# Gated attention and two expert mixtures on one core: the first mixture by 512 tokens in a written order, the early heads of a pair as one 128x128 block

## The chip, the core and the metric

One core of one Trainium2 chip runs the kernel. The metric is the device time of one execution in microseconds. Before the change the median of three runs is 990.67 us (990.52 to 990.67). One profiled execution took 989.96 us; the trace and all durations in this document come from it, or from the profiled execution of the kernel that is named.

## The reference

Three layers follow each other. The weights of the first mixture arrive as 64-bit floating-point words; the output is float32.

```python
# 1. gated linear attention: 4 batches, 8 heads, 768 tokens, 48 channels
for t in range(768):
    state = alpha[:, :, t, :, None] * state + k[:, :, t] (x) v[:, :, t]   # outer product
    y[:, :, t] = q[:, :, t] . state
x = y as 3072 tokens x 384
# 2. first mixture: 384 -> 768 -> 384
x = max(x @ w1, x @ w2, x @ w3) @ w_out
# 3. second mixture: 8 experts, the two best of each token
logits = x @ w_gate + log1p(exp(x @ w_noise)) * noise
out[token] += softmax weight * (relu(x @ w1[e]) @ w2[e])   # 384 -> 1024 -> 384
```

## The kernel before

**Attention.** A half unit j (24 of them) is 256 tokens of four heads: two pairs of heads, one head of a pair on partitions 0 to 47, the other on 64 to 111, with 16 padding partitions above each. The 256 tokens are four chunks of 64. `prep_a` runs two scans on VectorE over the decays (a reverse one for `kh`, then a forward one for `D`, which needs the reciprocals of the first) and GpSimd multiplies the keys; `prep_x` multiplies the queries by `D`, one VectorE operation for each height (`x1`, `x2`; L258, L259). `att_t` transposes the keys, `att_s` makes the scores and masks them with two VectorE multiplies (L293). `att_g` makes the outer sums in the bank `psG`, puts the last state into its column 0 (L311 clears it for the first in a sequence), scans over it (L316), multiplies by the decay (L319) and copies the states beside the values (`LA`, `LB`). `att_y` gets the outputs, two matmuls with 64 rows of output for each chunk, and splits them into a high and a low part (`xt`); six small DMAs (`xt<-sg`) fill the rows 48 to 63 and 112 to 127 of them.

**First mixture.** Two half units make a unit u of 256 tokens. `ffn(u, f)` does one of six blocks of 128 hidden channels: for each of three weights nine matmuls of 256 columns (three slices of the depth, each as high x high, high x low, low x high). The first two weights go into one bank (tag `p12`), the third into another (`p3`), two buffers of each. ScalarE copies the first (L366), VectorE takes two maxima (L367, L368), ScalarE and GpSimd split the result into `H`. `proj(u, t)` multiplies 128 tokens by `w_out` and by the gates (18 matmuls of 400 columns, `psl`). The weights come as 64-bit words; `wconv(i)`, twelve times, turns them into two float32 parts in `dissect`: ScalarE takes the absolute value (L163), VectorE does four operations (a maximum with a tiny number L164, a shift L165, and two that put sign and low bits in, L166 and L167), ScalarE and GpSimd make the high and low part (L169, L170). It uses two work tiles, `ca` and `cb`, with two buffers each.

**Second mixture.** `route_a` to `route_m` find the two experts of six tiles of tokens at a time (four batches) and write a table of token numbers. `eload` loads an expert's weights, `esplit` splits them (L738, L739), `gather` fetches rows by an indirect DMA, `turn` transposes them (L773) and copies them into `xe` (L775), `up` and `down` are the two products (L792 with 384 or 448 columns, L806 with 384), `scatter` adds the rows to the output by indirect DMA.

**What sets the order.** The calls stand in a written list in the code: the attention of the first units, the weight conversions and the first blocks one by one, then a loop over the units 3 to 11, then the last projections and the first expert. Within the reach of the list a scheduler with modelled times puts each engine's instructions in order, and the buffers of each tag bound how far it can move them. The calls between the last blocks of the first mixture and the third transpose of the expert's second part are called the handover here.

## Time and profile before

| | of the profiled execution |
|---|---|
| its own time; span of the trace | 989.96 us; 988.3 us |
| TensorE matmuls (PE), weight loads (PEld) | 913.0 us (92%), 866.7 us (88%) |
| VectorE (DVE) | 514.6 us (52%) |
| ScalarE (ACT) | 389.5 us (39%) |
| GpSimd (POOL) | 329.3 us (33%) |
| granted TensorE clock, mean of the span | 0.98 of 2.4 GHz |
| moved by DMA | 88.22 MB, mean 89 GB/s |

The span runs from the first instruction to the last; the 1.66 us that the execution takes beside it are not in the trace. An engine's busy share is an average over stages that have different limits. In the first 120 us TensorE is busy in 69.2 us and VectorE in 110.4, from 120 to 480 TensorE in 356.3 of 360 and VectorE in 236.3. So the table of stages is read before the shares.

### The profile page before, as it was taken

Reading aid. Unit: us, or ns where it says so; the run is one execution under the profiler, and the core shown is the slowest. Engines: PE = TensorE matmul, PEld = TensorE weight load, DVE = VectorE, ACT = ScalarE, POOL = GpSimd, SP = SyncE. Lnnn points to the kernel's source line nnn. Section 1 sums busy time; section 2 is a strip of 40 time slices with the busy share of each in tenths; the row PEclk is TensorE's granted clock in tenths of the full one; section 3 lists DMA queues with packets and bytes.
Section 4 is the critical chain, followed back from the end, with each engine's and each line's share of the span. In section 5 each row is a group of like instructions: output and inputs, shape, how many; then the busy total and the mean of one; then the engine's idle time right before and its main releaser. Section 6 shows DMA issues by size and latency. Waiting matters only on the chain.

```text
span 988.3 us, 17871 instructions
## 1 busy us (share of the span) xinstructions
PE 913.0 (92%) x7186; PEld 866.7 (88%) x7187; DVE 514.6 (52%) x1040; ACT 389.5 (39%) x801; POOL 329.3 (33%) x362
## 2 busy tenths in 40 slices
PE   2358999999999999999898999999999999999994
PEld 2347999999999999999897999999999999999993
DVE  7999847786668865772573333322333323333110
ACT  3645454455445534632542333332333332333220
POOL 5477524322322332112108333333333233221112
PEclk9979899999999999999999999999999999999998
DMA  9642223134234232104325444334434434422112
GB/s 266 171 137 70 60 55 87 46 106 121 57 82 122 75 81 64 31 13 137 139 87 123 113 105 101 78 79 115 110 98 108 94 60 109 113 57 25 21 25 29
DMA packets 36693, 88.22 MB, mean 89 GB/s; under 512 B 8640, under 2 KB 25024, under 8 KB 36608
## 3 DMA queue, kind: packets, MB, share of 16 engines
q1 hardware_dynamic: 25600, 66.39, 23.7%
q0 software_dynamic: 11008, 20.67, 12.0%
q8 instruction: 57, 0.93, 0.4%
q14 instruction: 28, 0.23, 0.1%
HBM read 64.52 MB, written 20.16 MB: 86 GB/s over the span
## 4 chain that ended last, share of the span: by engine, by line
PE 74%; issue 4%; DMA 3%; DVE 2%; POOL 0%; ACT 0%; POOLq 0%; ACTq 0%; DVEq 0%
PE psd L806 21%; PE psu L792 21%; PE p L363 18%; PE psl L378 5%; DMA out_dram<-y,idx 2%; PE psx L773 2%; PE psS L290 1%; PE psG L306 1%; PE psY L331 1%; PE psT L282 1%; DMA xt<-sg 1%; PE psY L332 1%; DVE kh L239 0%; DVE x L259 0%; DMA xg<-x2d,idx 0%
## 5 line engine op out<-in xcount | busy, mean ns | idle before, releaser
L363 PE MATMUL p<-xt,W 128*128 128x256 f32 x1944 | 254.7, 289 | 9.9 <-DVE m L367 7.3
L363 PEld LDWEIGHTS p<-xt,W 128*128 128x128 f32 x1944 | 241.9, 195 | 15.0 <-DVE m L367 8.1
L792 PE MATMUL psu<-xe,ew 128*128 128x448 f32 (+1 forms) x1152 | 242.5, 358 | 4.3 <-ACT xe L775 4.3
L806 PE MATMUL psd<-ew,he 128*128 128x384 f32 (+1 forms) x1344 | 243.3, 335 | 0.0
L806 PEld LDWEIGHTS psd<-ew,he 128*128 128x128 f32 (+1 forms) x1344 | 227.0, 180 | 8.1 <-ACT y L809 0.2
L792 PEld LDWEIGHTS psu<-xe,ew 128*128 128x128 f32 x1152 | 208.2, 190 | 13.9 <-ACT xe L775 4.7
L796 DVE SCALAR_TENSOR_TENSOR he<-psu,he 128x448 fp32r<-128x448 f32 (+1 forms) x128 | 75.5, 590 | 265.0 <-ACT he L795 265.0
L811 POOL DMA_INDIRECT out_dram<-y,idx x56 | 88.1, 1573 | 187.8 <-ACT y L809 176.2
L371 POOL TENSOR_TENSOR H<-m,H 128x256 fp32r<-128x256 f32 x72 | 60.1, 835 | 191.2 <-ACT H L370 187.1
L809 ACT ACTIVATE y<-psd,GS 128x384 f32<-128x384 f32 (+1 forms) x56 | 32.4, 580 | 206.1 <-PE psd L806 195.2
L795 ACT ACTIVATE he<-psu 128x448 fp32r<-128x448 f32 (+1 forms) x128 | 66.3, 518 | 112.3 <-PE psu L792 112.3
L378 PE MATMUL psl<-WO,H 128*128 128x400 f32 x432 | 84.7, 349 | 0.0
L378 PEld LDWEIGHTS psl<-WO,H 128*128 128x128 f32 x432 | 76.7, 188 | 2.1 <-issue 1.3
L739 DVE TENSOR_TENSOR ew<-raw,ew 128x768 fp32r<-128x768 f32 x64 | 57.2, 954 | 33.6 <-ACT ew L738 32.9
L758 POOL DMA_INDIRECT xg<-x2d,idx x56 | 58.5, 1045 | 43.2 <-PE psx L773 21.2
L367 DVE TENSOR_TENSOR m<-p,m 128x256 f32<-128x256 f32 x72 | 29.9, 417 | 60.4 <-ACT m L366 59.9
L370 ACT CAST H<-m 128x256 fp32r<-128x256 f32 x72 | 29.2, 406 | 68.0 <-DVE m L368 66.2
L777 POOL COPY GS<-xg 128x1 f32<-128x1 f32 (+1 forms) x56 | 10.8, 272 | 124.2 <-DMA xg<-x2d,idx 124.2
L366 ACT COPY m<-p 128x256 f32<-128x256 f32 x72 | 26.4, 369 | 61.6 <-PE p L363 58.4
L738 ACT CAST ew<-raw 128x768 fp32r<-128x768 f32 x64 | 48.6, 831 | 3.2 <-DMA raw<-in_e_dram 3.2
L331 PE MATMUL psY<-x,la 128*64 128x64 f32 x384 | 31.5, 237 | 15.6 <-ACT la L321 14.9
L331 PEld LDWEIGHTS psY<-x,la 128*64 128x64 f32 x384 | 27.1, 148 | 19.7 <-ACT la L321 15.7
(151 smaller groups left out, 1080.0 us busy)
## 6 DMA issues: line engine op xcount, KB each, us to landing
raw<-in_e_dram SPq DMA_DIRECT2D x32, 768.0 KB, 5.6
qka<-in_qka_dram SPq DMA_DIRECT2D x48, 289.7 KB, 4.7
out_dram<-z SPq DMA_DIRECT2D x5, 960.0 KB, 4.5
vn<-in_vn_dram SPq DMA_DIRECT2D x24, 192.0 KB, 2.6
x2d<-x2t SPq DMA_DIRECT2D x24, 192.0 KB, 1.9
RAW<-in_ws_dram SPq DMA_DIRECT2D x5, 768.0 KB, 10.8
wraw<-in_ws_dram SPq DMA_DIRECT2D x4, 768.0 KB, 8.6
xt<-sg SPq DMA_DIRECT2D x72, 32.0 KB, 3.5
```

Of the source, the lines that this page charges most:

```text
L331: nc.tensor.matmul(ps[0:64, p, s], LA[i][:, p, c], X1[j][:, sx], start=True, stop=True)
L363: nc.tensor.matmul(ps, W[:, f, w, a, k], x[:, k, b], start=n == 0, stop=n == 8)
L371: nc.gpsimd.tensor_sub(H[:, u % 2, f, 1], m, hi.bitcast(F32))
L378: nc.tensor.matmul(ps, H[:, u % 2, f, a, 128 * t:128 * t + 128], WOT[0][:, b, f], start=n == 0, stop=n == 17)
L738: nc.scalar.copy(hi, r)
L739: nc.vector.tensor_sub(EW[e, m][:, 1, s], r, hi.bitcast(F32))
L758: nc.gpsimd.indirect_dma_start(out=XG[n, i][0:w], out_offset=None, in_=x2d if h else x2d[0:128 + LATE], in_offset=bass.IndirectOffsetOnAxi ...
L792: nc.tensor.matmul(ps, w[:, a, f, k], XE[n][:, k, b], start=i == 0, stop=i == 8)
L795: nc.scalar.activation(hi, ps, AF.Relu)
L796: nc.vector.scalar_tensor_tensor(HE[n][:, f, 1], ps, 0.0, hi.bitcast(F32), op0=OP.max, op1=OP.subtract)
L806: nc.tensor.matmul(ps, HE[n][:, f, a, o:o + m], w[:, b, f], start=j == 0, stop=j == 23)
L811: nc.gpsimd.indirect_dma_start(out=out, out_offset=bass.IndirectOffsetOnAxis(ap=IDX[h][0:m, 1, c:c + 1], axis=0), in_=y, in_offset=None, c ...
```

## The change

**Attention.** `EARLY = 4`: in the half units 0 to 3 the pair's two heads are one block. One tile `L[0]` holds the values, both heads on the diagonal, and one tile `L[1]` the states; an output chunk is two matmuls of 128 rows that add up in the bank (masked scores by values, decayed queries by states). So one multiply of full height makes the queries (L294 for L258 and L259), and one mask multiply the scores. In all half units the decay scan now starts from the decay of the last step (`Z[0]`) and comes first, the reverse scan second. `att_g` adds the old state into column 1 and one scan adds and multiplies, so the multiply by the decay goes; ScalarE spreads the factors `AE`. The inputs of the first two half units come as three pieces of columns with the padding inside (`qk2`), the decays first; the values have a load of their own (`load_v`).

**Weights.** The maximum of `dissect` moves to GpSimd, and the work tile is one, in place, with two buffers. Raw weights have other homes.

**First mixture.** `ffn(d, f, half)` works on groups of 512 tokens. Group 0 and the blocks 0 and 1 of group 1 run in halves of 256 columns, all else with 512. Each of a block's three products has a bank of its own, of one tag `p` with four buffers, which `up` uses too. `proj(d, t)` has four tiles of 128 tokens in a group.

**Routing and order.** Batches of 6, 6, 6, 2 and 4 tiles instead of four times 6. The order of the calls is written as two strings, in which `f1.0.1` is `ffn(1, 0, 1)` and `r` one step of the routing; at the handover a third string sets it and the scheduler does not move TensorE, VectorE and ScalarE.

```diff
+EARLY = 4
+BATCH = (0, 6, 12, 18, 20, 24)
+HANDOVER = """
+    L0.0.0 L0.0.1 L0.1.0 G0.0 G0.1 G0.2 E0.0.0 E0.0.1 p5.0 E0.0.2 E0.0.3 p5.1 T0.0 T0.1 T0.2 E0.1.0 E0.1.1
...
+ORDER = """
+    a0 x0 t0 a1 s0 v0 g0 x1 s1 a2 t1 y0 v1 x2 g1 a3 y1 w0 v2 w1 w2 t2 s2 x3 g2 v3 w3 w4 t3 s3 y2 g3 a4
...
     def load(j):
         i = j % 2
-        for g in range(2):
-            nc.sync.dma_start(QKA[i][64 * g:64 * g + 48], qka[j, g])
-        nc.sync.dma_start(VN[i].rearrange("p a b c e -> p (a b c e)"), vn[j])
+        if j < 2:
+            for a, b in ((1024, 1545), (512, 1024), (0, 512)):
+                nc.sync.dma_start(QKA[i][:, a:b], qk2[j, :, a:b])
...
     def dissect(raw, hi, lo):
-        a = at.tile([128, 768], U32, tag="ca", name="ca", bufs=2)
-        b = at.tile([128, 768], F32, tag="cb", name="cb", bufs=2)
+        b = cv.tile([128, 768], F32, tag="cb", name="cb", bufs=2)
+        a = b.bitcast(U32)
         nc.scalar.activation(b, high.bitcast(F32), AF.Abs)
-        nc.vector.tensor_scalar(b, b, TINY, None, op0=OP.max)
-        nc.vector.tensor_scalar(a, b.bitcast(U32), 5, 2, op0=OP.logical_shift_left, op1=OP.logical_shift_right)
+        nc.gpsimd.tensor_scalar(b, b, TINY, None, op0=OP.max)
+        nc.vector.tensor_scalar(a, a, 5, 2, op0=OP.logical_shift_left, op1=OP.logical_shift_right)
...
     def prep_a(j):
+        nc.vector.tensor_copy(Z[0][:, 0:512:64], a0)
+        D = DD[j] = at.tile([128, 512], F32, tag="D", name="D")
+        nc.vector.tensor_tensor_scan(D, al[:, 0:512], Z[0], 0.0, op0=OP.mult, op1=OP.add)
+        nc.vector.reciprocal(Z[1][:, 63:512:64], D[:, 63:512:64])
         R = KH[j] = at.tile([128, 512], F32, tag="kh", name="kh", bufs=2)
-        nc.vector.memset(Z[:, 0:512:64], 1.0)
-        nc.vector.tensor_tensor_scan(R[:, ::-1], al[:, 512:0:-1], Z, 0.0, op0=OP.mult, op1=OP.add)
-        nc.vector.reciprocal(Z[:, 0:512:64], R[:, 0:512:64])
-        D = DD[j] = at.tile([128, 512], F32, tag="D", name="D")
-        nc.vector.tensor_tensor_scan(D, al[:, 0:512], Z, 0.0, op0=OP.mult, op1=OP.add)
-        r0 = at.tile([128, 2, 4], F32, tag="r0", name="r0")
-        nc.gpsimd.tensor_copy(r0.rearrange("p a b -> p (a b)"), R[:, 0:512:64])
+        nc.vector.tensor_tensor_scan(R[:, ::-1], al[:, 512:0:-1], Z[1][:, ::-1], 0.0, op0=OP.mult, op1=OP.add)
         nc.gpsimd.tensor_mul(R, t[:, 512:1024], R)
-        nc.gpsimd.tensor_mul(AE[i][:, :, :, 1:5],
-                             a0.rearrange("p (a b) -> p a b", a=2)[:, :, None, :].to_broadcast([128, 2, 48, 4]),
-                             r0[:, :, None, :].to_broadcast([128, 2, 48, 4]))
+        EN[j] = at.tile([128, 2, 4], F32, tag="en", name="en", bufs=2)
+        nc.vector.tensor_copy(EN[j].rearrange("p a b -> p (a b)"), D[:, 63:512:64])
...
+    def bank(j, name, early=False):
+        if early and j < 4:
+            return pm.tile([128, 512], F32, tag="p", name=name, bufs=4)
+        return pa.tile([128, 512], F32, tag="a", name=name)
...
     def att_s(j):
+        if j < EARLY:
+            nc.vector.tensor_mul(X2[j].rearrange("p (c t) -> p c t", c=8), ps.rearrange("p (c t) -> p c t", c=8),
+                                 mask[:, None, :].to_broadcast([128, 8, 64]))
+            return
...
     def att_g(j):
+        nc.scalar.copy(AE[:, :, :, 1:5], EN[j][:, :, None, :].to_broadcast([128, 2, 48, 4]))
...
+        nc.vector.memset(ps[:, :, :, 0], 0.0)
+        if not first:
+            before = ST[j - 2][:, :, :, 4]
+            nc.scalar.copy(LA[i][64:128, :, 0, 0:48], before[64:128])
+            nc.scalar.copy(LB[i][0:64, :, 0, 0:48], before[0:64])
+            nc.vector.tensor_add(ps[:, :, :, 1], ps[:, :, :, 1], before)
+        nc.vector.tensor_tensor_scan(st.rearrange("q p e c -> q (p e c)"), ps.rearrange("q p e c -> q (p e c)"),
+                                     AE.rearrange("q p e c -> q (p e c)"), 0.0, op0=OP.add, op1=OP.mult)
-        nc.vector.tensor_mul(st[:, :, :, 0:4], st[:, :, :, 0:4], AE[i][:, :, :, 1:5])
...
+    def att_y_mm(j):
+                for k, X in enumerate((X2, X1)):
+                    nc.tensor.matmul(ps[:, p, sc], L[k][:, p, c], X[j][:, sx], start=k == 0, stop=k == 1)
...
-    def ffn(u, f):
-        p12 = pm.tile([128, 2, 256], F32, tag="p12", name="p12")
-        p3 = pm.tile([128, 2, 256], F32, tag="p3", name="p3")
+    def ffn(d, f, half=None):
+        s = slice(0, 512) if half is None else slice(256 * half, 256 * half + 256)
+        x = XT[d][:, :, :, s]
+        m = pw.tile([128, 512], F32, tag="m", name="m", bufs=2)[:, s]
+        for w in range(3):
+            ps = pm.tile([128, 512], F32, tag="p", name="p", bufs=4)[:, s]
...
+            if w == 0:
+                nc.scalar.copy(m, ps)
+            else:
+                nc.vector.tensor_max(m, ps, m)
...
+    with tc.manual_schedule(engines={mybir.EngineType.PE, mybir.EngineType.DVE, mybir.EngineType.Activation}):
+        run(HANDOVER)
```

VectorE from its 20th instruction or so on, when the first weights are converted; a row gives the line, the operation, and output<-input with their shape (`cb` and `ca` are the work tiles, `x` the queries or masked scores, `st` the states). Before:

```order
L164 TENSOR_SCALAR cb<-cb 128x768
L293 TENSOR_TENSOR x_155<-psS,mask 64x512
L293 TENSOR_TENSOR x_156<-psS,mask 64x512
L165 TENSOR_SCALAR ca<-cb 128x768
L311 MEMSET psG 128x96
L164 TENSOR_SCALAR cb<-cb 128x768
L166 SCALAR_TENSOR_TENSOR ca<-wraw,ca 128x768
L316 SCALAR_TENSOR_TENSOR st<-ae_105,psG 128x480
L165 TENSOR_SCALAR ca<-cb 128x768
L167 SCALAR_TENSOR_TENSOR ca<-wraw,ca 128x768
L164 TENSOR_SCALAR cb<-cb 128x768
L319 TENSOR_TENSOR st<-st,ae_105 128x96x4
```

The same place after:

```order
L294 TENSOR_TENSOR x_209<-qka_99,D 128x512
L340 TENSOR_TENSOR x_149<-psS,mask 128x512
L368 MEMSET psG 128x96
L375 SCALAR_TENSOR_TENSOR st<-psG,ae 128x480
L208 TENSOR_SCALAR cb<-cb 128x768
L209 SCALAR_TENSOR_TENSOR cb<-RAWH,cb 128x768
L340 TENSOR_TENSOR x_210<-psS,mask 128x512
L210 SCALAR_TENSOR_TENSOR cb<-RAWH,cb 128x768
L208 TENSOR_SCALAR cb<-cb 128x768
L209 SCALAR_TENSOR_TENSOR cb<-RAWH,cb 128x768
L210 SCALAR_TENSOR_TENSOR cb<-RAWH,cb 128x768
```

A conversion has three operations there instead of four, the mask is one row of full height, and the multiply of the states has gone.

TensorE at the handover, from the last blocks of the first mixture (`p`, L363) over the last projections (`psl`), the transposes (`psx`) and the first expert's products (`psu`, `psd`). Before:

```order
L363 MATMUL p_5828<-xt,W 128x256 x9
L378 MATMUL psl_5879<-WO,H 128x400 x3
L378 MATMUL psl_5902<-WO,H 128x400 x15
L773 MATMUL psx<-ident,xg 128x128 x6
L378 MATMUL psl_5925<-WO,H 128x400 x18
L378 MATMUL psl_5955<-WO,H 128x400 x18
L773 MATMUL psx<-ident,xg 128x128 x3
L792 MATMUL psu<-xe_5988,ew 128x384 x36
```

The same place after, up to the routing's first matmul (`psr`):

```order
L466 MATMUL psl_5017<-WO,H 128x400 x11
L466 MATMUL psl_5047<-WO,H 128x400 x18
L728 MATMUL psx<-ident,xg 128x128 x9
L466 MATMUL psl_5099<-WO,H 128x400 x18
L466 MATMUL psl_5128<-WO,H 128x400 x18
L747 MATMUL psu<-xe_5070,ew 128x384 x27
L538 LDWEIGHTS tri
L538 MATMUL psr<-r_ob,tri 128x32
```

All nine transposes stand ahead of the last two projections there, and the routing's matmuls come after the third up block. Further down, before the second part's transposes:

```order
L610 MATMUL pstab<-r_C,r_A 128x192
L747 MATMUL psu<-xe_5070,ew 128x384 x9
L761 MATMUL psd<-ew,he_5183 128x384 x48
L728 MATMUL psx<-ident,xg 128x128 x6
L761 MATMUL psd<-ew,he_5183 128x384 x24
L728 MATMUL psx<-ident,xg 128x128 x3
```

The eighth up block and two down blocks stand between the routing's last matmul (`pstab`, into the table of token numbers) and the next transposes.

## Rows read from the trace of the kernel before

**Rows 1.** Stages: window, us, busy (count) PE, PEld, DVE, ACT, POOL, clock, DMA, GB/s.
```profile
0.00:60.00 60.00, 22.14 (x251) 19.61 (x253) 52.92 (x70) 28.03 (x49) 33.28 (x44) 0.94 0.75 204
60.00:120.00 60.00, 47.06 (x463) 44.35 (x462) 57.48 (x76) 29.06 (x60) 38.74 (x28) 0.86 0.31 79
120.00:480.00 360.00, 356.27 (x3743) 339.83 (x3742) 236.31 (x567) 163.97 (x375) 103.82 (x127) 1.00 0.29 75
480.00:540.00 60.00, 52.94 (x291) 48.84 (x290) 34.69 (x115) 26.17 (x51) 18.06 (x26) 0.94 0.46 137
540.00:960.00 420.00, 420.00 (x2363) 400.75 (x2362) 133.15 (x215) 139.97 (x264) 129.28 (x136) 1.00 0.37 84
```
**Rows 2.** Timeline, VectorE, 8 to 15 us: start, us, operation, idle before.
```profile
8.57 1.23 DVE L239 TENSOR_TENSOR_SCAN kh<-qka,Z 128x512 f32<-128x512 f32 x1 [5.22 <-DMA qka<-in_pad_dram]
10.07 1.23 DVE L242 TENSOR_TENSOR_SCAN D<-qka,Z 128x512 f32<-128x512 f32 x1
```
**Rows 3.** Groups, VectorE, 0 to 111 us: busy us, mean ns, idle before.
```profile
L242 DVE TENSOR_TENSOR_SCAN D<-qka,Z 128x512 f32<-128x512 f32 x7 | 13.3, 1902 | 0.1
L165 DVE TENSOR_SCALAR ca<-cb 128x768 uint32<-128x768 uint32 x11 | 8.5, 776 | 0.0
L166 DVE SCALAR_TENSOR_TENSOR ca<-wraw,ca 128x768 uint32<-128x768 uint32 x6 | 8.1, 1359 | 0.0
L164 DVE TENSOR_SCALAR cb<-cb 128x768 f32<-128x768 f32 x11 | 8.0, 723 | 0.0
L259 DVE TENSOR_TENSOR x<-qka,D 64x512 f32<-64x512 f32 x6 | 7.9, 1309 | 0.1
L258 DVE TENSOR_TENSOR x<-qka,D 64x512 f32<-64x512 f32 x6 | 7.0, 1173 | 0.2
L293 DVE TENSOR_TENSOR x<-psS,mask 64x512 f32<-64x512 f32 x10 | 6.8, 682 | 0.1
L316 DVE TENSOR_TENSOR_SCAN st<-ae,psG 128x480 f32<-128x480 f32 x5 | 5.7, 1141 | 0.1
L167 DVE SCALAR_TENSOR_TENSOR ca<-wraw,ca 128x768 uint32<-128x768 uint32 x6 | 5.7, 944 | 0.0
L319 DVE TENSOR_TENSOR st<-st,ae 128x384 f32<-128x384 f32 x5 | 4.5, 892 | 0.0
L240 DVE RECIPROCAL Z<-kh 128x8 f32<-128x8 f32 x7 | 1.4, 196 | 0.1
```
**Rows 4.** Chain of work that ended last: start, us, what.
```profile
347.99 5.97 DMA xt<-sg
...
460.12 19.45 PE p L363 x162
...
655.74 4.18 PE psd L806 x24
659.92 5.30 PE psu L792 x27
...
938.46 3.71 PE psu L792 x18
```
**Rows 5.** Groups, ScalarE, 0 to 111 us, columns as in rows 3.
```profile
L169 ACT CAST W<-ca 128x768 fp32r<-128x768 f32 x9 | 7.5, 835 | 8.2 <-DVE ca L167 8.1
L163 ACT ACTIVATE cb<-wraw 128x768 f32<-128x768 f32 x6 | 5.5, 910 | 2.0 <-DMA wraw<-in_ws_dram 2.0
```
**Rows 6.** Groups, GpSimd, 0 to 111 us, columns as in rows 3.
```profile
L170 POOL TENSOR_TENSOR W<-ca,W 128x768 fp32r<-128x768 f32 x9 | 19.4, 2166 | 16.7 <-ACT W L169 16.7
L247 POOL TENSOR_TENSOR ae<-qka,r 128x384 f32<-128x384 f32 x7 | 10.4, 1482 | 2.4 <-DVE Z L238 1.6 <-DVE st L319 0.5
```
**Rows 7.** Waits of TensorE, 440 to 560 us: us, count, longest.
```profile
PE psu L792 <- ACT xe L775: 4.3, 2, 3.9
```
**Rows 8.** Timeline, 35 to 41 us, columns as in rows 2.
```profile
36.80 1.99 POOL L245 TENSOR_TENSOR kh<-qka,kh 128x512 f32<-128x512 f32 x1
37.58 2.29 DVE L242 TENSOR_TENSOR_SCAN D<-qka,Z 128x512 f32<-128x512 f32 x1
```

More of the change, by code (lines that the diff above doesn't have):

```diff
@@ L105, in gla_moe_kernel @@
         load(i)
-        for g in range(2):
-            nc.sync.dma_start(QKA[i][64 * g + 48:64 * g + 64], pad)
+        load_v(i)
     for i in range(5):
         wload(i)
-    nc.vector.memset(Z, 0.0)
+    for z in Z:
+        nc.vector.memset(z, 0.0)
     nc.gpsimd.memset(ident, 1.0)
@@ L319, in att_g @@
[L319 to L339 removed]
+        first = (j // 2) % 3 == 0
@@ new lines, in att_g, with att_y @@
+        c = 0 if first else 1
+        nc.scalar.copy(LA[i][64:128, :, c:4, 0:48], P[64:128, :, c:4])
+        nc.scalar.copy(LB[i][0:64, :, c:4, 0:48], P[0:64, :, c:4])
+    YP = {}
+    def att_y(j):
+        att_y_mm(j)
+        att_y_lo(j)
+    def att_y_mm(j):
+        i, u = j % 2, j // 2
+        d, s = u // 2, slice(256 * (u % 2), 256 * (u % 2) + 256)
+        ps = YP[j] = pa.tile([128, 2, 256], F32, tag="a", name="psY")
+        for p in range(2 if j < EARLY else 0):
+            for c in range(4):
+                sc = slice(64 * c, 64 * c + 64)
+                sx = slice(256 * p + 64 * c, 256 * p + 64 * c + 64)
+                for k, X in enumerate((X2, X1)):
+                    nc.tensor.matmul(ps[:, p, sc], L[k][:, p, c], X[j][:, sx], start=k == 0, stop=k == 1)
+        for p in range(2 if j >= EARLY else 0):
+            for c in range(4):
+                sc = slice(64 * c, 64 * c + 64)
+                sx = slice(256 * p + 64 * c, 256 * p + 64 * c + 64)
+                nc.tensor.matmul(ps[0:64, p, sc], LA[i][:, p, c], X1[j][:, sx], start=True, stop=True)
+                nc.tensor.matmul(ps[64:128, p, sc], LB[i][:, p, c], X2[j][:, sx], start=True, stop=True)
+        if i == 0 and u % 2 == 0:
+            XT[d] = XW2[d % 2]
@@ L410, in route_b @@
         t, l = RT[b]
-        nl = NL[b]
-        u = small([128, 6, NE], "u")
-        d = small([128, 6, NE], "d")
+        n = BATCH[b + 1] - BATCH[b]
+        nl = NL[b][:, 0:n]
+        u = row("u", b, NE)
+        d = row("d", b, NE)
         nc.vector.tensor_scalar(u, t, 1.0, None, op0=OP.add)
@@ L465, in route_r @@
         xf, oh, rk, ct = RT[b]
-        rb = small([128, 6, NE], "rb")
+        n = BATCH[b + 1] - BATCH[b]
+        rb = row("u", b, NE)
         if b == 0:
@@ L511, in route_m @@
             A, C = held.pop(0)
-            nc.tensor.matmul(ps[:, 0:n], A, C[:, 0:n], start=q == 0 and i == 0, stop=q == 2 and i == 3)
-        if q < 2:
+            nc.tensor.matmul(ps[:, 0:n], A, C[:, 0:n], start=q == 0 and i == 0, stop=q == last and i == 3)
+        if q < last:
             return
@@ new lines, in gla_moe_kernel, with run @@
+    steps = []
+    CALL = {"a": prep_a, "x": prep_x, "v": prep_v, "t": att_t, "s": att_s, "g": att_g, "y": att_y, "w": wconv,
+            "f": ffn, "p": proj, "i": gates_t, "j": gates_m, "z": zero_rows, "c": late_consts}
+    def run(order):
+        for word in order.split():
+            if word == "r":
+                while steps and next(steps[0], steps) is steps:
+                    steps.pop(0)
+                continue
+            args = [int(n) for n in word[1:].split(".") if n]
+            CALL[word[0]](*args)
+            if word[0] == "p" and 4 * args[0] + args[1] + 1 in BATCH:
+                steps.append(routing(BATCH.index(4 * args[0] + args[1] + 1) - 1))
```

524 lines of the change are left out of this document (170 added, 354 removed).

## The prediction, made before the run

> **What bounds the kernel now.** I read the table of stages first: one line for each stretch of the span, with the busy time of each engine and the granted TensorE clock [rows 1]. TensorE is busy 356.27 of the 360 us from 120 to 480, and all 420 us from 540 to 960: there only less matmul work can shorten the run. It is idle for 60 - 22.14 = 37.9 us before 60 us, for 60 - 47.06 = 12.9 us from 60 to 120, and for 60 - 52.94 = 7.1 us from 480 to 540. In the first 120 us the busy engine is VectorE: 52.92 and 57.48 us of 60. The clock of these stretches is also lower, 0.94, 0.86 and 0.94 of the 2.4 GHz level, which says that part of them ran at 1.2 GHz: the lost matmul time is (1 - 0.94) x 60 = 3.6, 8.4 and 3.6 us, some of it inside the idle time.
>
> Then I read who is late. VectorE's first scan waits 5.22 us for the padding DMA [rows 2] and then has work without a break; the groups of VectorE up to 111 us, when it first waits again, are in [rows 3]. So the start is a backlog of VectorE, the middle is TensorE, and the handover has waits of its own: in it TensorE waits 4.3 us for the input copies of the first expert [rows 7].
>
> **The change part by part.** The profiled execution took 989.96 us for a span of 988.3, and the median of the runs is 990.67; the sum is made against 989.96.
>
> *512 columns in the first mixture.* 1944 matmuls of 256 columns become 1188. Group 0 (6 blocks) and two blocks of group 1 stay in halves: 8 x 2 x 27 = 432 at 256. The other 4 + 24 = 28 blocks make 28 x 27 = 756 at 512, each in place of two. No row shows 512 columns. From long runs in the chain [rows 4]: 162 of 256 in 19.45 us, 120 ns each; 24 of 384 in 4.18, 174 ns; 27 of 448 in 5.30, 196 ns; 18 of 448 in 3.71, 206 ns. A pair of 256 costs 240 ns. Carrying on the slope from 384 to 448 gives 196 + 22 = 218 ns by the first row and 206 + 32 = 238 by the second, so a pair saves 22 to 2 ns; the slope from 256 to 384 is 54/128 = 0.42 ns a column, and with it from 448 (about 201) I get 228. That saves 12 ns, and 756 x 12 = 9 us (bounds 1.5 and 16.5). It is all on the path, since most of it lies where TensorE is saturated.
> The Trainium skill ("TensorE: Matmul & The Clock Gate", Back-to-back issue gap) puts the gap between lone matmuls at the column count over 2.4 GHz plus 2.5 ns; that would be 109 against 216 ns, and a pair would save only 2 ns, 2 us in the sum. This trace disagrees at 256, where it shows 120 ns; were the rule to hold at 512 alone, the saving would be 24 ns and 18 us.
>
> *The start.* What leaves VectorE in the first 111 us [rows 3]: the maximum of each weight conversion goes to GpSimd (L164, 11 x 0.72 = 8.0 us); in the first four half units one full-height multiply stands for L258 and L259 (4 x 1.2 = 4.7) and one mask multiply for two of L293 (4 x 0.68 = 2.7); the multiply by the decay, L319, is folded into the scan (5 x 0.89 = 4.5). The first load comes as three column pieces with the decay columns first, and the pads inside; the scan needs only the first piece, so of the 5.2 us wait I take 4 off. Sum 23.9. Added: two copies of 128x8 per preparation, seven by 111 us, each between nothing and the 0.20 of L240, which has the same size (I take 0.15, nearer that row), 14 x 0.15 = 2.1. The clearing of one column and the addition of the old state stand where one copy stood, and a conversion keeps its three other operations, now in place. Net 22 us less for VectorE.
> Not all of it reaches TensorE. Before 60 us it is idle 37.9 us, so that what VectorE gains there counts; from 60 to 120 only 12.9 us are idle, and the new order has in this stretch more attention ahead of the feed-forward blocks. I take half: 11 us, with 22 as the upper bound. The lower bound is below nothing. In the early blocks three banks serve one block of 27 matmuls, out of four, so TensorE may run only two of them (2 x 9 x 120 = 2.2 us) ahead of VectorE's maximum, against four (4.3 us) before; with 16 such half blocks and 0.5 us each that is 8 us lost.
> On ScalarE there is one broadcast copy per half unit more (at most L169's 0.83 us at twice the size), hidden: it is busy 28 of 60 us there. The full-width matmuls of the state and the values in four half units load 128 weight columns instead of 64, 64 matmuls in all; half of them stand in the idle time before 60 us, and what is left, 32 matmuls, costs less than 120 ns each, under 3.9 us; I count it within the half not taken.
> *The conversions' chain.* The two work tiles become one with two buffers, so a third conversion waits for the first to leave GpSimd: ScalarE 0.91 [rows 5], maximum on GpSimd (between the 0.72 that VectorE takes for it and the 2.17 of GpSimd's L170, which has its size and two inputs [rows 6]; 1.3, as it has one), VectorE 0.78 + 1.36 + 0.94, ScalarE 0.83, GpSimd 2.17: 8.3 us for two, 4.1 each, 50 us for twelve. Today they are spread over more than 90 us of VectorE's backlog, which hides this; uncovered at single places it costs 2 to 3 us, again within the half not taken.
>
> *The handover.* In the order before, the last three projections and their transposes stand between the last feed-forward block and the first expert matmul, and ScalarE's copy xe stands in its queue behind casts of weights. In the new order ScalarE has the three copies before the second weight's casts, and four projections cover them. The last batch of routing has four tiles for six, and its gathers stand ahead of the eighth up block and the first two down blocks, which are 9 x 0.174 + 48 x 0.174 = 9.9 us of matmuls before the first transposes of the next part. Idle time and lost clock are 7.1 + 3.6 = 10.7 us, the upper bound. The new order also puts the routing's matmuls after the third up block, so TensorE may wait there for VectorE's chain; I take 4 to 5 of the 10.7 as kept, and 6 as gained. Lower bound -2, if the routing is late by more than what goes.
>
> *At no cost.* ScalarE's further copies and the one batch more of routing, beside engines under 60% busy from 120 to 480 [rows 1]; the expert stage is the same work.
>
> Sum: 9 + 11 + 6 = 26; 989.96 - 26 = 964.
>
> **The rivals.**
> *B: VectorE's time comes back as waiting.* GpSimd is given up to twelve maxima. A VectorE operation with both inputs in SBUF is stretched when GpSimd works: the scan L242 took 2.29 us beside GpSimd's L245 [rows 8], against 1.23 where it stands alone [rows 2]; over the stretch its mean is 1.90. 12 x 1.3 = 15.6 us of maxima replace L247's 10.4 us and the small copies, so the stretching may rise as much as the work falls. Then the start gains nothing: 989.96 - 9 - 6 = 975. Against it: the removed L247 weighs nearly as much as what comes.
> The Trainium skill ("SBUF — State Buffer", Who interferes with whom) says that the two engines share a port pair under an exclusive lock, for VectorE operations with two SBUF inputs among others. By that rule the trace agrees (2.29 against 1.23).
> *C: all of it arrives.* TensorE follows VectorE in full and the middle of the bounds is too low: 14 + 20 + 9 = 43, so 947. For it: TensorE's idle time before 60 us alone is 37.9. Against: from 60 us on it can't gain more than it idles.
> *D: slower, by the ends of the 512-token groups.* A group's first matmul needs four half units instead of two, with the little DMAs that complete their rows. The chain shows one of these at 5.97 us [rows 4]; with the two masks, the scan and two copies of the last half unit before it (2 x 0.68 + 1.14 [rows 3], 2 x 0.83 [rows 5]: 4.2) a boundary could stand open for 10 us, at four boundaries 40: 964 + 40 = 1004. It decides from 26 us, 6.5 us at each boundary. Against: today's eleven boundaries cost less than the 3.7 us of idle time between 120 and 480 together, and in the new order projections and the next half unit's scores stand in between.
> *E: the change doesn't do what it says.* Two 256 cost what 512 cost, and the start and handover only shift: 988.
>
> **How the numbers follow.** A change of under 0.2%, 2 us, can't be told from none here. Chances: forecast 0.52 (own range 955 to 973), B 0.20, C 0.12, D 0.08, E 0.08. Faster: 0.52 + 0.20 + 0.12 and a third of E, 0.87; the same: the rest of E, 0.05; slower: D, 0.08. The range from 946 to 984 holds the forecast, B and about half of C; D, E and the other half, 0.2, are outside. The single time is the forecast's 964.
>
> **What would show it.** Long runs of 512-column matmuls at 225 to 231 ns (218 or 238 would move the sum by 8 us). TensorE idle up to 120 us at about 40 instead of 50.8 us, VectorE's first scan before 5 us, the first feed-forward maximum earlier than now, and L242's successor with a mean not over 1.9 us; a mean well above, with GpSimd busier, is B. Between 480 and 540 less than 3 us idle. Wrong would be: waits of over 5 us at the first matmul of a 512 group (D), TensorE idle in the first 120 us unchanged with VectorE still without a break (B), or VectorE itself waiting for GpSimd's maximum or for TensorE by more than 8 us in the start.

## The result, and the profile after

The changed kernel takes 975.94 us (median of four runs, 974.94 to 977.83): 0.9842 of the time before, 95% interval 0.9821 to 0.9862. A later series gave 0.9842 again (0.9829 to 0.9855). The median before, now of four runs, is 990.67 us still; by the two medians alone the ratio is 0.985. The gain is about 15 us. The forecast was 26 us, 964; the time lies in the stated range, and two of the three terms were too large.

The stages after, with the columns of [rows 1]:

```profile
0.00:60.00 60.00, 29.81 (x298) 26.81 (x300) 53.72 (x70) 31.98 (x56) 43.82 (x40) 0.76 0.68 212
60.00:120.00 60.00, 53.10 (x536) 50.35 (x536) 54.87 (x79) 37.04 (x80) 39.41 (x25) 0.93 0.34 87
120.00:480.00 360.00, 355.67 (x2942) 304.40 (x2941) 230.36 (x555) 173.31 (x373) 73.89 (x67) 1.00 0.31 81
480.00:540.00 60.00, 54.21 (x304) 51.52 (x303) 32.32 (x103) 23.18 (x46) 23.30 (x34) 0.97 0.46 126
540.00:960.00 420.00, 419.49 (x2360) 399.46 (x2358) 125.10 (x203) 134.56 (x254) 128.07 (x128) 1.00 0.37 79
```

TensorE idles 60 - 29.81 + 60 - 53.10 = 37.1 us up to 120 us, 13.7 less than before. Its busy time rose by as much, from 69.2 to 82.9 us, so that the idle time alone shows no gain. From 480 to 540 it idles 5.8 us against 7.1. VectorE's busy time up to 120 us is 108.6 us against 110.4: it still works nearly without a break.

The clock column of the first stage, 0.76 here and 0.94 in [rows 1], can't be compared. A stretch ahead of the trace's first clock record counts there as full clock, and the records begin at 13.7 us after and only at 47.2 us before. The matmuls tell the level. Four transposes of keys before, in a window whose column says 1.00:

```profile
0.00:47.00 47.00, 14.90 (x178) 12.71 (x180) 40.01 (x54) 22.21 (x39) 22.45 (x39) 1.00 0.84 226
```

```profile
24.96 1.09 PE L282 MATMUL psT<-ident,kh 128*128 128x128 f32 x4 [1.28 <-DVE st L316]
```

The same operation after, ahead of the first record and just behind it, where full clock is on record:

```profile
8.54 1.12 PE L329 MATMUL psT<-ident,kh 128*128 128x128 f32 x4 [8.54 <-POOL kh L283]
...
14.40 0.66 PE L329 MATMUL psT<-ident,kh 128*128 128x128 f32 x4
```

So TensorE ran at 1.2 GHz ahead of the first record too. With the stretch ahead of it counted, the half clock lasts some 54 of the first 60 us before and 43 after: the clock of this start is low in both kernels, and not lower after the change.

Two events bound the part that got shorter. Timeline of TensorE, the first matmul of the first mixture and the first of the experts, before:

```profile
55.30 1.01 PE L363 MATMUL p<-xt,W 128*128 128x256 f32 x3
...
494.21 3.15 PE L792 MATMUL psu<-xe,ew 128*128 128x384 f32 x9 [3.89 <-ACT xe L775]
```

The same two after, and the routing's first matmul behind them:

```profile
61.30 0.99 PE L451 MATMUL p<-xt,W 128*128 128x256 f32 x3
...
478.69 4.91 PE L747 MATMUL psu<-xe,ew 128*128 128x384 f32 x27
487.55 0.19 PE L538 MATMUL psr<-r_ob,tri 128*128 128x32 bf16 x1 [3.95 <-DVE r_ob L527]
```

The experts start 15.5 us earlier, and the span is 15.0 us shorter (988.3 and 973.3): nothing was won behind that point. The first mixture starts 6 us later than before, not earlier; its first maximum on VectorE comes at 71.90 us against 71.74.

What was won ahead of the first expert matmul can be split, since the clock from 120 us to there is on record as full in both. Up to 120 us, from there to that matmul, and behind it (columns of [rows 1]), before:

```profile
0.00:120.00 120.00, 69.20 (x712) 63.97 (x714) 110.39 (x145) 57.08 (x108) 72.02 (x72) 0.90 0.53 142
120.00:494.21 374.21, 366.59 (x3803) 349.82 (x3801) 245.60 (x579) 174.64 (x397) 104.57 (x128) 1.00 0.30 82
494.21:988.30 494.09, 477.19 (x2674) 452.91 (x2674) 158.55 (x318) 157.80 (x297) 152.66 (x162) 0.98 0.37 82
```

and after:

```profile
0.00:120.00 120.00, 82.91 (x832) 77.17 (x834) 108.59 (x148) 69.01 (x136) 83.23 (x64) 0.84 0.51 150
120.00:478.69 358.69, 354.36 (x2935) 303.09 (x2934) 229.28 (x554) 172.00 (x371) 73.89 (x67) 1.00 0.31 80
478.69:973.30 494.61, 475.01 (x2669) 452.29 (x2668) 158.51 (x306) 159.29 (x301) 153.26 (x162) 0.99 0.38 84
```

In the middle stretch TensorE has 366.59 - 354.36 = 12.2 us less to do and idles 4.3 us instead of 7.6; the 3.3 us are mostly the wait of 3.89 in front of the first expert matmul, which has gone. Of the 12.2 us the wider matmuls make about 9.5 (below), so that the start is only 2 to 3 us further at 120 us. Behind the first expert matmul 2.7 us more of idle time stand against 2.2 us less of busy time. Together that is 12.2 + 3.3 - 0.5 = 15.0 us. It is one execution of each kernel; in a second one of the changed kernel (**again**, below) the first expert matmul comes at 479.16 us.

The first mixture's matmuls are where most of the gain is; the page's groups, before and after (busy us, mean ns, idle before):

```profile
L363 PE MATMUL p<-xt,W 128*128 128x256 f32 x1944 | 254.7, 289 | 9.9 <-DVE m L367 7.3
```

```profile
L451 PE MATMUL p<-xt,W 128*128 128x512 f32 (+1 forms) x1188 | 245.2, 360 | 4.6 <-DVE m L456 4.5
```

That is 9.5 us. Most of TensorE's added work in the first 120 us is in the attention's outputs: the tile `psY` in the first 120 us (columns of [rows 1] without GpSimd), before and after:

```profile
0.00:120.00 120.00, 9.32 (x160) 8.13 (x160) 3.01 (x6) 3.19 (x7) 0.90 0.53 142
```

```profile
0.00:120.00 120.00, 21.40 (x192) 20.31 (x192) 4.10 (x8) 3.97 (x9) 0.84 0.51 150
```

12.1 us more of TensorE, for 32 rows more (one half unit). The groups of VectorE and GpSimd up to 111 us after, columns as in [rows 3]:

```profile
L208 DVE TENSOR_SCALAR cb<-cb 128x768 uint32<-128x768 uint32 x12 | 13.5, 1125 | 3.1 <-POOL cb L207 2.8
L209 DVE SCALAR_TENSOR_TENSOR cb<-RAW,cb 128x768 uint32<-128x768 uint32 x7 | 12.0, 1716 | 0.1
L279 DVE TENSOR_TENSOR_SCAN D<-qka,Z 128x512 f32<-128x512 f32 x8 | 10.5, 1315 | 0.1
...
L285 DVE COPY en<-D 128x8 f32<-128x8 f32 x8 | 4.4, 552 | 0.0
L277 DVE COPY Z<-qka 128x8 f32<-128x8 f32 x9 | 4.0, 441 | 1.0 <-DMA qka<-in_qk_dram 0.8
```

```profile
L207 POOL TENSOR_SCALAR cb<-cb 128x768 f32<-128x768 f32 x12 | 30.7, 2557 | 5.7 <-ACT cb L206 5.6
```

By 111 us VectorE has done eight decay scans and twelve shifts, where it had done seven (L242) and eleven (L165) [rows 3]: it is about one half unit and one conversion further. A maximum takes 2.56 us on GpSimd, where VectorE took 0.72 [rows 3]. The conversion's shift, 0.776 us before (L165), takes 1.125. The timeline of VectorE shows that shift alone and beside GpSimd, whose subtraction L213 ran from 43.17 for 1.79 us; ahead of them the first scan:

```profile
3.96 1.22 DVE L279 TENSOR_TENSOR_SCAN D<-qka,Z 128x512 f32<-128x512 f32 x1
...
18.71 0.55 DVE L208 TENSOR_SCALAR cb<-cb 128x768 uint32<-128x768 uint32 x1
...
43.23 2.15 DVE L208 TENSOR_SCALAR cb<-cb 128x768 uint32<-128x768 uint32 x1 [2.02 <-POOL cb L207]
```

### The profile page after: what moved, and what is told of

It is laid out like the page before. It is cut to its first block, busy times and chain, and to the rows that moved or that the text cites. A ratio compares the mean times of both kernels' runs of the same rounds, so it can differ in the third digit from the quotient of the medians.

```text
span 973.3 us, 16241 instructions
## 1 busy us (share of the span) xinstructions
PE 912.3 (94%) x6431; PEld 832.5 (86%) x6432; DVE 496.4 (51%) x1006; ACT 400.3 (41%) x806; POOL 310.4 (32%) x293
## 4 chain that ended last, share of the span: by engine, by line
PE 79%; DVE 8%; DMA 4%; ACT 3%; issue 2%; POOL 2%; SPq 0%; POOLq 0%; DVEq 0%; ACTq 0%
PE psd L761 22%; PE psu L747 22%; PE p L451 21%; PE psl L466 6%; DMA out_dram<-y,idx 2%; PE psx L728 2%; PE psY L402 2%; PE psS L337 1%; POOL cb L207 1%; DMA qka<-in_qka_dram 1%; PE psG L361 1%; DVE D L279 1%; DVE cb L210 1%; PE psT L329 1%; ACT l L307 1%
## 5 line engine op out<-in xcount | busy, mean ns | idle before, releaser
L451 PE MATMUL p<-xt,W 128*128 128x512 f32 (+1 forms) x1188 | 245.2, 360 | 4.6 <-DVE m L456 4.5
L451 PEld LDWEIGHTS p<-xt,W 128*128 128x128 f32 x1188 | 195.9, 192 | 36.4 <-DVE m L456 4.9
L456 DVE TENSOR_TENSOR m<-p,m 128x512 f32<-128x512 f32 (+1 forms) x88 | 51.7, 589 | 48.3 <-PE p L451 41.4
L459 POOL TENSOR_TENSOR H<-m,H 128x512 fp32r<-128x512 f32 (+1 forms) x34 | 41.0, 1209 | 110.0 <-ACT H L458 109.9
L466 PE MATMUL psl<-WO,H 128*128 128x400 f32 x336 | 68.3, 348 | 0.0
L283 POOL TENSOR_TENSOR kh<-qka,kh 128x512 f32<-128x512 f32 x24 | 33.3, 1388 | 105.5 <-DVE kh L282 37.0
L466 PEld LDWEIGHTS psl<-WO,H 128*128 128x128 f32 x336 | 60.1, 188 | 1.6 <-issue 0.5
L458 ACT CAST H<-m 128x512 fp32r<-128x512 f32 (+1 forms) x34 | 18.5, 544 | 52.6 <-DVE m L456 52.5
L344 DVE TENSOR_TENSOR x<-psS,mask 64x512 f32<-64x512 f32 x40 | 27.4, 686 | 23.0 <-PE psS L338 22.5
L337 PEld LDWEIGHTS psS<-x,kh 64*64 64x64 f32 x384 | 27.2, 146 | 13.9 <-DVE x L294 7.7
```

The lines of the kernel that those rows point to most:

```text
L451: nc.tensor.matmul(ps, W[:, f, w, a, k], x[:, k, b], start=n == 0, stop=n == 8)
L456: nc.vector.tensor_max(m, ps, m)
L459: nc.gpsimd.tensor_sub(lo, m, hi.bitcast(F32))
L466: nc.tensor.matmul(ps, place(d, f)[:, a, 128 * t:128 * t + 128], WOT[0][:, b, f], start=n == 0, stop=n == 17)
```

## The experiments

A difference of two ratios to the kernel before, times 991 us, is the difference in time. The first seven change one thing in the changed kernel; early2, reord, halfbanks and cols stand on autohand.

**w256: two runs of 256 columns for one of 512.**

```diff
+            for q in range(0, ps.shape[1], 256):
...
-                    nc.tensor.matmul(ps, W[:, f, w, a, k], x[:, k, b], start=n == 0, stop=n == 8)
+                        nc.tensor.matmul(ps[:, q:q + 256], W[:, f, w, a, k], x[:, k, b, q:q + 256],
+                                         start=n == 0, stop=n == 8)
```

> Each product of 512 columns as two runs of nine matmuls with 256 columns, in the same bank and the same order of blocks. Theory 1, the 512 columns are worth what the rows show: 756 x (240 - 227 ns) = 9.8 us, all on the path, 985 to 986.5. Theory 2, what the groups of 512 gain comes from fewer and longer blocks (fewer waits at their ends), not from the matmuls: 976 to 979.

986.70 us, ratio 0.9950 (0.9936 to 0.9964): 10.7 us slower. Longest runs in the chain of waits (start, us, what), first of the changed kernel and then of w256:

```profile
418.06 12.26 PE p L451 x54
```

```profile
407.56 26.11 PE p L452 x216
```

227 ns for 512 columns and 121 for 256. Theory 1 holds: the width is worth 10.7 us, 0.9 more than 756 x 13 ns.

**maxdve: the maximum back on VectorE.**

```diff
-        nc.gpsimd.tensor_scalar(b, b, TINY, None, op0=OP.max)
+        nc.vector.tensor_scalar(b, b, TINY, None, op0=OP.max)
```

> The maximum of each weight conversion goes back from GpSimd to VectorE, all else as in the changed kernel (975.94 us, span 973.3). Theory 1, GpSimd's price: up to 111 us the twelve maxima take 30.7 us there, 2.56 each, and beside them VectorE's shift takes 1.13 us a time where it takes 0.55 alone, and the next operation 1.6 where it takes 0.96. Back on VectorE they cost 12 x 0.72 = 8.7 us, and give back 12 x 0.58 + 12 x 0.6 = 14: VectorE gains some 5 us up to 111 us, the first feed-forward matmul comes at about 56 us instead of 61.3, and the time is 970 to 973. Theory 2, VectorE's amount of work bounds the start: 8.7 us more of it, half of which arrives, 979 to 981, with VectorE busier up to 120 us than the 108.6 us of now.

979.52 us, ratio 0.9866 (0.9847 to 0.9885): 2.4 us slower, at the edge of what the intervals separate. Its stretches up to the first expert matmul, and two of its VectorE groups up to 111 us:

```profile
0.00:120.00 120.00, 85.85 (x768) 80.51 (x770) 107.60 (x153) 64.96 (x126) 48.89 (x51) 0.74 0.52 147
120.00:484.34 364.34, 359.48 (x3002) 308.27 (x2999) 234.93 (x561) 176.08 (x380) 74.74 (x68) 1.00 0.31 80
```

```profile
L207 DVE TENSOR_SCALAR cb<-cb 128x768 f32<-128x768 f32 x12 | 8.6, 718 | 2.4 <-ACT cb L206 2.3
...
L208 DVE TENSOR_SCALAR cb<-cb 128x768 uint32<-128x768 uint32 x12 | 8.2, 687 | 0.2
```

VectorE is busy 107.6 us up to 120 us, with 8.6 us of maxima, as against 108.6 without them. Since it has hardly a gap in either kernel, this doesn't say what the move is worth; how far it got does. Beside its 12 maxima it did 141 operations here, and 148 in the changed kernel. By the mean times of their groups the seven are some 5 us of work (an estimate), 1 us of it from the longer busy time; so about 4 of the 8.6 us were gained by the move, and the rest came back as stretched operations (the shift alone 13.5 - 8.2 = 5.3 us, while other operations are shorter). TensorE has 359.5 us of work left at 120 us up to the first expert matmul, instead of 354.4. Theory 1 is wrong in its sign. The time is theory 2's; the longer busy time of VectorE that it forecast can't show where VectorE has no gap. The two profiled executions are the slowest of five here and the fastest of four there, so the 2.4 us of the medians are the size to go by.

**early0: no 128x128 blocks.** The edit is `EARLY = 0`.

> EARLY = 0: the first four half units use the 64-row matmuls and half-height multiplies like the others. Theory 1, TensorE pays: the 64 matmuls of 128x128 appear as 128 rows in the trace, 112 ns apart at full clock and 213 at half, 14 to 27 us, and would be 64 rows of pairs 58 ns apart, 4 to 7 us; since TensorE has only 37 us idle up to 120 us, part of it is on the path, and the time falls by 2 to 5 us, to 971 to 974. Theory 2, VectorE pays: it gets 4 x 0.5 us for the queries and 4 x 0.68 for the masks, 4.8 us more, of which half or all arrives: 978 to 981.

978.65 us, ratio 0.9871 (0.9850 to 0.9892): 2.9 us slower, theory 2. Its `psY` in the first 120 us:

```profile
0.00:120.00 120.00, 10.88 (x192) 8.76 (x192) 4.05 (x8) 3.92 (x9) 0.86 0.52 151
```

TensorE does get 10.5 us back (21.40 to 10.88), as theory 1 said, and idles 8.8 us longer up to 480 us (29.80, 48.09 and 351.84 us busy in the first three stages): the blocks are worth their price, by 3 us and not by the 7.4 us (4.7 and 2.7) that the prediction takes off VectorE for them. What they cost on TensorE stands mostly in time in which it would wait.

**foldback: the states' multiply back on VectorE, by ones.**

```diff
+        nc.vector.tensor_mul(st[:, :, :, 0:4], st[:, :, :, 0:4], ONE.to_broadcast([128, 2, 48, 4]))
         c = 0 if first else 1
```

> After each state scan VectorE multiplies the states by ones, in place, an operation of the size of the one that the change took away (0.89 us); it stands on the chain to the states. Theory 1, half of VectorE's work in the start arrives: seven by 111 us, 6.3 us, of which 3: the time is 978 to 980. Theory 2, VectorE's work is not what sets the start any more: 975.5 to 977. Theory 3, all arrives: 981 to 983.

986.08 us, ratio 0.9940 (0.9924 to 0.9956): 9.7 us slower, more than theory 3, though the operation takes only 0.55 us here. Its stretch from 120 us up to the first expert matmul, and a wait of TensorE there (us, times, longest) that the changed kernel has not:

```profile
120.00:487.93 367.93, 357.92 (x2955) 306.88 (x2954) 240.24 (x577) 176.57 (x378) 76.48 (x68) 1.00 0.30 79
```

```profile
PE p L454 <- DMA xt<-sg: 2.3, 2, 1.7
```

TensorE idles 10.0 us there instead of 4.3. The operation stands in the chain from the state scan over ScalarE's copies to the outputs, and this chain is close to late in the middle too. The other part lies in the start: TensorE has 357.9 us of work left at 120 us, instead of 354.4. Up to the first expert matmul the two parts are 5.7 and 3.6 us, in one execution of each kernel.

**handover: projection and routing ahead of the last two casts.**

```diff
-    p5.2 E0.1.2 E0.1.3 p5.3 A4 B4 U0.0 U0.1 U0.2 C4 R4 U0.3 H4.0
+    p5.2 p5.3 A4 B4 E0.1.2 E0.1.3 U0.0 U0.1 U0.2 U0.3 C4 R4 H4.0
```

> At the handover the fourth projection and the first routing steps come before the last two casts of the second weight, and the routing's matmul after the fourth up block instead of the third. Now TensorE waits 3.95 us for VectorE there and 1.38 us before the first up block of the second part. Theory 1, the chain copy of the logits, exponentials, VectorE sets that wait: it starts some 2.5 us earlier and has 1.6 us more cover, so 3.9 us go, and the time is 971.5 to 972.5, with less than 0.5 us of wait before the routing's matmul. Theory 2, the wait is taken over by the casts that now come late, or by ScalarE's copies of the up blocks: 975 to 977, with a new wait of 2 to 4 us before a down block or an up block.

976.75 us, ratio 0.9846 (0.9832 to 0.9861): no change, theory 2. Waits of TensorE from 440 to 560 us, of the changed kernel and of handover:

```profile
PE psr L538 <- DVE r_ob L527: 4.0, 1, 4.0
PE psu L747 <- ACT xe L730: 1.4, 1, 1.4
```

```profile
PE psu L747 <- DVE he L751: 3.1, 1, 3.1
PE psu L747 <- ACT xe L730: 1.2, 1, 1.2
PE psr L538 <- DVE r_ob L527: 1.0, 1, 1.0
```

The wait for the routing became one for VectorE's work on the up blocks.

**autohand: the scheduler orders the handover.**

```diff
-    with tc.manual_schedule(engines={mybir.EngineType.PE, mybir.EngineType.DVE, mybir.EngineType.Activation}):
-        run(HANDOVER)
+    run(HANDOVER)
```

> The same calls at the handover, but the scheduler sets the order of TensorE, VectorE and ScalarE. Theory 1, the written order is worth what the rows show, some 1 us (6.8 us of idle TensorE after 463 us against 7.1 before): 976 to 978. Theory 2, the written order is what keeps the handover at 6.8 us and the scheduler would do worse: over 980, with TensorE idle for over 10 us from 463 to 520.

974.90 us, ratio 0.9828 (0.9815 to 0.9841), 1.4 us less by the ratios than the control of the same series (**again**, the changed kernel, 976.74 us). Its five times, 974.49 to 975.72, hardly meet those of the control, 975.44 to 979.89, but the two intervals overlap. TensorE is busy 56.79 of the 60 us from 480 to 540. Waits, same view:

```profile
PE psx L728 <- DMA xg<-x2d,idx: 2.0, 3, 0.8
PE psu L747 <- ACT xe L730: 0.9, 2, 0.5
```

Both theories miss: the written order does not help, and the wait of 3.95 us comes from it; that it costs 1 to 2 us of the time is likely, but not clear of noise. In the profile of the control the wait for `xe` is 3.6 us instead of 1.4, so these waits differ between executions of one kernel too. What was expected of the control:

> The changed kernel itself, as a control beside the others of this series. All theories: a ratio of 0.984 to before, within 0.002; the granted clock of the first 120 us may differ from the first profile, since the four variants so far showed 24 to 55 us of half clock there against 38.

**warm: transposes of the identity in TensorE's waits.**

```diff
+    WARM = {"t2": 24, "t3": 10, "s3": 40, "y1": 20}
...
+        for i in range(WARM.get(name, 0)):
+            nc.tensor.transpose(ps, ident, ident)
```

> 94 transposes of the identity stand where TensorE waits in the start: 20 before the second unit's outputs (wait 3.96 us), 24 and 10 before the third and fourth transposes of keys (4.31 and 1.61), 40 before the fourth scores (7.41). Their results are overwritten; they are 10 us of work at 108 ns each. Theory 1, the half clock makes the start long: with the waits filled there are under 15 us of half clock up to 120 us instead of 37.5, the matmuls between the waits go twice as fast, the first feed-forward matmul comes at 57 to 59 us instead of 61.3, and the time is 970 to 973. Theory 2, VectorE and GpSimd set the start: the clock rises but the first feed-forward matmul stays at 61 us, 975 to 977. Theory 3: the fillers overrun the waits, 978 to 981.

982.18 us, ratio 0.9897 (0.9879 to 0.9914): 5.5 us slower, just above theory 3's range. Its first two stages:

```profile
0.00:60.00 60.00, 42.82 (x400) 40.17 (x402) 51.97 (x68) 32.92 (x58) 40.90 (x40) 0.80 0.73 220
60.00:120.00 60.00, 52.58 (x545) 49.35 (x544) 53.65 (x80) 36.27 (x80) 38.17 (x24) 0.97 0.35 85
```

The clock rose by 0.04 only; with the stretch ahead of the first record counted as half clock, the half clock up to 120 us fell from 51 to 39 us, far from theory 1's condition. So the run does not decide between theories 1 and 2.

**early2: blocks in two half units.** `EARLY = 2`, on autohand.

> EARLY = 2, and the scheduler orders the handover as in autohand (974.9 us), with which this is compared. Only the half units 0 and 1, which lie in TensorE's idle time, keep the 128x128 blocks. Theory 1, the heavy output matmuls of the half units 2 and 3 stand on TensorE's path: its psY time (42.6 us up to the first up block in autohand, 30.8 with EARLY = 0) falls by 5 to 6 us, VectorE gets 2 x 0.5 + 2 x 0.68 = 2.4 us more, and the time is 971 to 973.5. Theory 2, VectorE's operations on the chain to the states and outputs decide there too: 975.5 to 977.5.

974.84 us, ratio 0.9834 (0.9820 to 0.9849): the same as autohand, neither theory's time. The blocks of the half units 2 and 3 neither gain nor cost.

**reord: another order of the start.** In this kernel the first half unit's outputs take the second's values and states; counts and shapes stay.

```diff
-    a0 x0 t0 a1 s0 v0 g0 x1 s1 a2 t1 y0 v1 x2 g1 a3 y1 w0 v2 w1 w2 t2 s2 x3 g2 v3 w3 w4 t3 s3 y2 g3 a4
-    x4 v4 y3 f0.0.0 w5
+    a0 x0 t0 a1 s0 v0 g0 x1 s1 t1 v1 g1 y0 y1 a2 w0 v2 w1 x2 w2 t2 s2 a3 g2 x3 v3 w3 w4 f0.0.0 t3 s3 y2 g3 a4
+    x4 v4 y3 w5
```

> Beside the handover as in autohand (974.9 us), the written order of the start has the second half unit's transposes, states and outputs ahead of the third decay scans and the first conversion, and the first feed-forward block ahead of the fourth keys' transposes. Now VectorE's second state scan starts at 31.9 us, though its matmuls ended at 21; the split of the second outputs ends at 54 and the first feed-forward matmul comes at 61. Theory 1, the order of VectorE's queue at the start is what keeps TensorE waiting: state scan before 26 us, first feed-forward matmul at 48 to 54, TensorE idle for 4 to 8 us less up to the first up block, and 968 to 972. Theory 2, what comes earlier is waited for elsewhere (weights of the next blocks, the third and fourth half unit): the first feed-forward matmul comes earlier, but TensorE's idle time falls by less than 2 us, 973.5 to 976.

978.76 us, ratio 0.9875 (0.9859 to 0.9891): 4.7 us slower than autohand. Its first stages, and two places of TensorE's timeline, the second the first matmul of the first mixture:

```profile
0.00:60.00 60.00, 36.06 (x280) 33.33 (x282) 52.88 (x67) 30.55 (x54) 42.56 (x40) 1.00 0.71 220
60.00:120.00 60.00, 48.78 (x515) 45.59 (x513) 52.76 (x75) 35.03 (x75) 33.10 (x22) 0.97 0.29 74
```

```profile
26.75 13.06 PE L397 MATMUL psY<-x,l 128*128 128x64 f32 x60 [3.97 <-ACT l L379]
...
55.22 1.01 PE L451 MATMUL p<-xt,W 128*128 128x256 f32 x3 [0.58 <-DMA xt<-sg]
```

The same instruction of `psY` in the changed kernel, where full clock is on record:

```profile
16.57 3.56 PE L397 MATMUL psY<-x,l 128*128 128x64 f32 x30 [1.34 <-ACT l L379]
```

The first mixture starts 6 us earlier and TensorE then idles 11.2 us from 60 to 120, as against 6.9 in the changed kernel and 4.9 in autohand: theory 2's mechanism, with a larger price. The 1.00 of the first stage is no full clock: the first clock record of this trace stands at 60.5 us. A row of `psY` takes 218 ns ahead of it, against 119 in the changed kernel, and three matmuls of the first mixture 1.01 us, against 0.59 in cols (below). So TensorE ran at 1.2 GHz through the whole first 60 us, and the slower clock is a rival for part of the 4.7 us that this run can't tell from theory 2.

**halfbanks: two banks for a half block.**

```diff
+            if half is None or w != 1:
+                bk = pm.tile([128, 512], F32, tag="p", name="p", bufs=4)
+            ps = bk[:, s] if half is None else bk[:, 256 * (w % 2):256 * (w % 2) + 256]
```

> A half block's first two products share one bank, as before the change, so that it takes two of the four banks and not three; the handover as in autohand (974.9 us). Theory 1, the 16 half blocks wait for banks as the lower bound of the prediction has it (8 us, of which rows show one wait of 4.5 us before p): TensorE's idle time falls by 2 to 5 us, 970 to 973. Theory 2, the half blocks wait for VectorE's work or for weights, not for banks: 974 to 976.

978.17 us, ratio 0.9871 (0.9851 to 0.9890): slower than autohand by 4.3 us. TensorE's wait for VectorE's maximum, from 0 to 150 us, is still there, and longer than autohand's 2.3 us:

```profile
PE p L453 <- DVE m L458: 4.2, 3, 2.1
```

Fewer banks for a half block gain nothing. Since two products then also share one bank, the run doesn't show that banks bound nothing at all; why sharing a bank costs 4 us stays open.

**cols: the blocks as pairs of 64 output rows.**

```diff
-                    nc.tensor.matmul(ps[:, p, sc], L[k][:, p, c], X[j][:, sx], start=k == 0, stop=k == 1)
+                    for o in (0, 64):
+                        nc.tensor.matmul(ps[o:o + 64, p, sc], L[k][:, p, c, o:o + 64], X[j][:, sx],
+                                         start=k == 0, stop=k == 1)
```

> The handover as in autohand (974.9 us, ratio to before 0.9828). In the half units 0 to 3 each 128x128 matmul of the outputs becomes two with 64 output rows and the same 128 rows of depth, side by side in the array; VectorE's full-height operations stay. By the rows the present ones stand 112 ns apart (128 rows, 14.3 us at full clock), and pairs with 64 output rows stand 58 ns apart: 128 such pairs, 7.4 us. Theory 1, TensorE's price for the blocks is on the path: its psY time up to the first up block falls from 42.6 to some 35 us, the idle time stays near 30 us, and the time is 968 to 972. Theory 2, these matmuls lie in waits for VectorE, GpSimd and ScalarE: psY falls, the idle time rises by as much, 973.5 to 976.

973.64 us, ratio 0.9817 (0.9803 to 0.9830), the fastest of all: 2.5 us below the changed kernel, of which autohand has 1.4; the 1.1 us to autohand are within the intervals. `psY` in the first 120 us, and the first matmul of the first mixture:

```profile
0.00:120.00 120.00, 17.62 (x320) 14.84 (x320) 4.54 (x9) 3.96 (x9) 0.89 0.54 153
```

```profile
51.23 0.59 PE L453 MATMUL p<-xt,W 128*128 128x256 f32 x3 [2.38 <-DMA xt<-sg]
```

The first mixture starts 10 us earlier and `psY` costs 5.9 us less than in autohand (23.55 us), but up to the first expert matmul TensorE idles 3.5 us longer (42.5 and 39.0), and the time lies at theory 2's lower end: most of that was cover for other waits.

## Why the prediction was right and where its sizes were wrong

*512 columns.* 9 us forecast; the rows show 9.5 and the experiment 10.7. The slope from 256 to 384 columns, carried on from 448, gave 228 ns, and 227 were measured. Rival E falls with it.

*The start.* 11 us forecast, 2 to 3 measured: 12.2 us less work for TensorE from 120 us on, less the 9.5 of the width. The step that failed is VectorE's "net 22 us less", half of which was taken; its costs were too low. The maximum on GpSimd is 2.56 us and not 1.3, above the upper bound of 2.17 that came from a row of the same size. VectorE's operations beside it are stretched, for which the sum had nothing; in maxdve about half of the maxima's 8.6 us come back that way. And the copies of 128x8 are 0.55 and 0.44 us and not 0.15, 8.4 us for 17 of them. What is left brought VectorE about one half unit and one conversion further by 111 us. Mis-sized too is the term on the full-width matmuls, "64 matmuls in all", half in idle time, the rest "under 3.9 us": a matmul there is two rows in the trace, and `psY` takes 10.5 us more in the first 120 us than with the same rows in early0. That this took the start's gain is not shown: taking the blocks away makes the kernel slower (early0), or no faster (early2), and cheaper rows bring little (cols).

Two signs came as forecast, the first scan at 3.96 us (before 5) and a mean of the decay scan of 1.3 us (not over 1.9). The first maximum, forecast earlier than before, is 0.2 us late. TensorE's 37.1 us of idle time, close to the 40 forecast, confirm nothing, because its busy time took up the 13.7 us. The time lies outside the forecast's own 955 to 973, and in the stated range because that takes in rival B. The prediction also reads the 0.94 of the first 60 us as 3.6 us of lost matmul time, where TensorE ran at 1.2 GHz for most of them; no term of the sum hangs on that reading.

*Rival B* named this mechanism and its time, 975, is the one measured. About half of it is shown, by maxdve. That the times agree is partly luck: B has nothing for the start and 6 us for the handover, and the runs show 2 to 3 for each; and the sign that was to be B's, a decay scan well above 1.9 us, did not come. The stretching also reached an operation with one input (the shift, 0.55 to 2.15 us), which the rival had left out. "SBUF — State Buffer" of the Trainium skill (Who interferes with whom) names `tensor_scalar` among the operations that can enter a two-port mode and then contend with GpSimd; the trace agrees, 0.55 us alone and 2.15 beside it.

The Trainium skill ("GPSIMD Engine Reference", Engine selection) calls one-input element-wise operations on GpSimd "roughly line-rate". The trace disagrees: 2.56 us there against 0.72 on VectorE for the same maximum.

*The fold.* It was counted at 4.5 us before 111 us, half of it, and at nothing later. foldback puts 9.7 us on it, of which 5.7 are waits behind 120 us. Counting VectorE's operations up to 111 us only, since it has gaps later (236 of 360 us busy [rows 1]), was the wrong measure for an operation on a chain that feeds a saturated TensorE.

*The handover.* 6 us forecast, 2 to 3 measured: 3.3 us of idle time less ahead of the first expert matmul, 0.5 us lost behind it. The risk that the text named, TensorE waiting for VectorE's chain at the routing's matmul, cost 3.95 us, and took the place of the 3.9 us that went in front of the first up block; what is left is 2.2 us less busy time behind it, where the granted clock is 0.99 instead of 0.98. Idle time from 480 to 540 is 5.8 us and not under 3. In autohand it is 3.2, so the written order, not the work, keeps the difference.

*Rival C* needed the start's whole 20 and the handover's 9. *Rival D* fell: no wait before a matmul of a 512 group reaches 5 us, and TensorE's idle time from 120 to 480 is 4.3 us against 3.7.

Undoing single parts costs 10.7, 9.7, 2.9 and 2.4 us, 25.7 together, while the whole change gains 15. Without the width that is 15 us undone against some 5 gained. The parts feed one chain, so they need not add up; but the new order of the calls, the loads and the tile in place were not undone by themselves, and some of the 10 us may be lost there. What holds the start back beyond the costs named stays open.

## What to carry to other kernels

Price an operation that goes to another engine, or takes another shape, on both engines: with what it costs where it goes, and with what it does to the operations beside it. Measure a saturated engine by how far it got, not by its busy time. An operation in the chain to a saturated engine can cost more late in the run than in the start, however idle its own engine is on average. And an order written by hand is to be run against the scheduler's, since the wait that it removes tends to come back one instruction later. Before a clock column is compared, look where its records begin; the time of equal matmuls tells the level without them.
